# Attention and two expert layers: bias rows of 640 columns, fewer and respaced loads, and products of the identity in the first pair

## The chip, the core and the metric

One Trainium2 chip, one core. The metric is the device time of one launch in microseconds, the median over runs. Engines: TensorE (PE; PEld is its weight load), VectorE (DVE), ScalarE (ACT), GpSimd (POOL) and SyncE (SP), which here issues every DMA.

## What is computed

Attention with a bias made from relative positions, then two expert layers on the 2304 rows that it gives.

```python
# B, H, S, D = 4, 8, 576, 64; hidden 32
scores = q @ k.T / sqrt(D)
x = log1p(abs(i - j)) / log1p(max(i, 1))
bias = relu(x * w1 + b1) @ w2                   # [S, S, H], the same for every batch
attn = softmax(scores + bias) @ v
x = rows of attn                                # [B*S, H*D] = [2304, 512]
h = x @ w_in;  x = (h - tanh(h)) @ w_out        # 512 -> 2048 -> 512
out = (silu(x @ w_gate) * (x @ w_val)) @ w_out2 # 512 -> 1536 -> 512
```

## The kernel before

**Bias tables.** The bias depends on the position and the head alone, so it is made once, in 36 tiles (`bias_rows`, L146). A tile holds 16 positions x 8 heads on 128 partitions and 576 columns. Four operations make the hidden rows `r` (`bias_hidden`, L128): three on VectorE (L141), one on ScalarE (L143). TensorE multiplies them by `w2` (L163, L168), ScalarE evicts the tile into `bev` (L172, scaled; there are five `bev` buffers), and SyncE writes it to DRAM scratch (L177). The order of tiles is written out (`GEN_ORDER`): the last 64 positions come first. Once all tiles of a span of positions are made, and two more, `bias_load` (L179) reads them back, for a pair of heads, as a tile `bt` of 128 partitions x 2 x 576. The columns of the second head are turned by 64 (512 to 575 come first), so its row is read in two pieces; a span takes three DMAs.

**Pairs and units.** The work goes through 16 pairs (two heads, one batch) of five units (128 positions; the first unit of a pair, t = 4, has 64). `load` (L194) brings q, k and v of a pair in quarter rows of 64 numbers, with the last 64 positions in a tile `end`: three issues for q, six for k, four for v. `qk_transpose` (L223) turns q and k on TensorE, ScalarE copies the result out (L245, L250, L253) and q and k are split into a high and a low part (`qk_high`, ScalarE, L269; `qk_low`, GpSimd, L60).

**A unit.** Scores on TensorE (L306), softmax: bias and minimum on VectorE (L321), exponential on ScalarE (L332), `r` = 1/sum on VectorE (L341, L342; one buffer), scaling on GpSimd (L350). Three units later the probabilities are transposed (L372, L389) and copied out (L402); values are multiplied in L421 into the PSUM bank `x`, which the last four table tiles also use (banks a, b, c and x).

**The order** is written out. After the tables' first part (33 tiles; `run`, L440, where a list `extra` puts one piece of the first two pairs' loading and transposing ahead of each two tiles), each unit is a step, and strings give the order of a step's pieces on every engine: C is scores, S softmax, G a table tile, P and p transposes, V values, F and D copies out, N and M the norm and scaling, L the loads. Pair n's q and k are loaded at step 5n-9, its v at step 5n+1. SyncE issues in program order.

**Expert layers.** Weight pieces are loaded as raw words and prepared (class `Weights`). During attention this goes in rounds of ten steps (`ALONE_PARTS`, L706): `W` is `vector_second`, which ends by issuing the next load (L597). The expert layers are products of two-part numbers, three per product (L695).

Of the kernel before, what the change touches and what calls it, by code (L numbers as in the profile page):

```python
# [9 lines left out]
F32 = mybir.dt.float32  # L10
# [36 lines left out]
)  # L47
AV_END = {(0, 0): (6, (0, 1, 2, 3, 4)), (1, 0): (7, (0, 1, 2, 3, 4))}

FIRST_ORDER = "LuCpQSOGPqVFoGDNME"  # L50
STEP_ORDER = "LuXYCHSTGGPpVFDNME"
FOURTH_ORDER = "LuCHSTPpVFXDNYME"
END_ORDER = "NMuPpFDAuPpFDVXY"

LAG = 3
GEN_ORDER = [G for t in TORDER for G in range(8 * t, min(8 * t + 8, NG))]


# [4 lines left out]
class Attention:  # L63
# [34 lines left out]
    def bias_setup(self):  # L98
        nc = self.nc
        c = self.gen_p  # L100
        self.ident = self.const.tile([128, 128], F32, name="ident")
        make_identity(nc, self.ident)
        self.cst = c.tile([128, NCONST], F32, name="cst")
        nc.sync.dma_start(out=self.cst[:, TABW:NCONST], in_=self.packed[:, TABW:NCONST])
        half = 640
        nc.sync.dma_start(out=self.cst[:, 0:half], in_=self.packed[:, 0:half])
        nc.sync.dma_start(out=self.cst[:, half:TABW], in_=self.packed[:, half:TABW])
        b1c = self.cst[:, C_B1:C_B1 + 1]
        self.b1p = c.tile([128, NBLK], F32, name="b1p")
        nc.vector.tensor_scalar(self.b1p, self.cst[:, C_PSI:C_PSI + NBLK], b1c, None, ALU.mult)  # L110
        self.table(self.cst[:, 0:half])
        self.rest = self.cst[:, half:TABW]

        self.w2 = self.cst[:, C_W2:NCONST]
        self.nipsi = c.tile([128, NG], F32, name="nipsi")
        rows = self.packed.rearrange("(g r) c -> g r c", g=QG)
        blocks = c.tile([128, NBLK], F32, name="blocks")
        for j in range(4):
            at = slice(32 * j, 32 * j + 32)
            nc.sync.dma_start(out=blocks[at, :], in_=rows[:, 0:H, C_NIPSI:C_NIPSI + NBLK])  # L120
            nc.gpsimd.tensor_copy(self.nipsi[at, :], blocks[at, j::4])
        self.scratch = [self.dram.tile([n * H, S], F32, name=f"bias_{t}") for t, (_, n) in enumerate(SPANS)]

    def table(self, t):

# [20 lines left out]
    def bias_rows(self, G):  # L146

        nc = self.nc
        n = GEN_ORDER.index(G)
        if n == 0:  # L150
            self.bias_hidden(G)
        if n + 1 < NG:
            self.bias_hidden(GEN_ORDER[n + 1])
        R = self.R.pop(G)
        if self.ps_gen:
            both = (self.ps_gen if n % 2 else self.ps_s).tile([128, 2, 512], F32, tag="s", name=f"bps_{G}")
            ps = both[:, 0, :], both[:, 1, :]
        else:
            both = None
            ps = [self.bank(tag, f"bps{tag}_{G}") for tag in ("cx" if n % 2 else "ab")]  # L160

        for j in range(4):
            nc.tensor.matmul(  # L163
                ps[0][32 * j:32 * j + 32].rearrange("p (t n) -> p n t", t=4), self.w2,
                R[j][:, 0:512].rearrange("p (n t) -> p n t", t=4), start=True, stop=True,
            )
        for j in range(4):
            nc.tensor.matmul(ps[1][32 * j:32 * j + 32, 0:64], self.w2, R[j][:, 512:S], start=True, stop=True)  # L168
        out = self.gen_p.tile([128, S], F32, tag="bev", name=f"bev_{G}", bufs=BEV_BUFS)
        ni = self.nipsi[:, G:G + 1]  # L170
        if both is not None:
            nc.scalar.activation(out, both.rearrange("p e n -> p (e n)")[:, 0:S], AF.Copy, scale=ni)  # L172
        else:
            nc.scalar.activation(out[:, 0:512], ps[0], AF.Copy, scale=ni)  # L174
            nc.scalar.activation(out[:, 512:S], ps[1][:, 0:64], AF.Copy, scale=ni)
        t, r0 = divmod(G, 8)
        nc.sync.dma_start(out=self.scratch[t][128 * r0:128 * r0 + 128, :], in_=out)  # L177

    def bias_load(self, hp, t):  # L179
        n = SPANS[t][1]  # L180
        bt = self.bias_p.tile(
            [128, n // 64, S], F32, tag=f"bias{n}", name=f"bt_{hp}_{t}", bufs=4 if n == 128 else 1,
        )
        src = self.scratch[t].rearrange("(q h) k -> q h k", h=H)

        for j in range(2):
            to = bt[:, j, :] if n == 128 else bt[64 * j:64 * j + 64, 0, :]
            for x, y, z in ((0, S, 0),) if j == 0 else ((64, S, 0), (0, 64, 512)):
                self.nc.sync.dma_start(out=to[:, x:y], in_=src[:, 2 * hp + j, z:z + y - x])
        self.bias_t[hp, t] = bt  # L190


# [1 line left out]
    def load(self, hp, b, nm):  # L194
        nc = self.nc
        a = {"q": self.q, "k": self.k, "v": self.v}[nm][b, 2 * hp:2 * hp + 2]
        t = self.nat.tile([128, 4, 2, D], F32, tag=nm, name=f"{nm}n_{hp}_{b}", bufs=2 if nm == "v" else 1)
        by4 = lambda j, x, y: a[j, x:y].rearrange("(p t) d -> p t d", t=4)
        for j in range(1 if nm == "k" else 2):
            nc.sync.dma_start(out=t[:, 0:4, j, :], in_=by4(j, 0, 512))  # L200
        if nm == "v":

            end = self.vend[self.nbuf["v"] % 2]
            self.nbuf["v"] += 1
            for j in range(2):
                nc.sync.dma_start(out=end[64 * j:64 * j + 64, j, :], in_=a[j, 512:576])
            self.nt[hp, b, nm] = t, end
            return

        if nm == "q":  # L210
            self.nt[hp, b, "end"] = self.nat.tile([128, 2, D], F32, tag="end", name=f"qkn_{hp}_{b}")
        end = self.nt[hp, b, "end"]
        if nm == "q":
            nc.sync.dma_start(out=end[64:128], in_=a[:, 512:576].rearrange("j p d -> p j d"))
        else:
            nc.sync.dma_start(out=end[0:64, 0, :], in_=a[0, 512:576])
            nc.sync.dma_start(out=t[0:64, 0, 1, :], in_=a[1, 512:576])
            nc.sync.dma_start(out=t[64:128, 0:4, 1, :], in_=by4(1, 0, 256))
            nc.sync.dma_start(out=t[0:64, 1:4, 1, :], in_=by4(1, 256, 512)[:, 0:3])
            nc.sync.dma_start(out=end[0:64, 1, :], in_=by4(1, 256, 512)[:, 3])  # L220
        self.nt[hp, b, nm] = t

    def qk_transpose(self, hp, b, which):  # L223

# [2 lines left out]
        ps = self.ps_s.tile([128, 2, 512], F32, tag="s", name=f"{which}T_{hp}_{b}")  # L227
        parts = [(slice(t, 256, 4) if which == "q" else slice(64 * t, 64 * t + 64), nat[:, t, :, :]) for t in range(4)]
        if which == "k":
            parts.append((slice(256, 320), self.nt.pop((hp, b, "end"))))  # L230
        for to, a in parts:
            for h in range(2):
                r = slice(64 * h, 64 * h + 64)
# [145 lines left out]
    def ends_t(self, u):  # L379
# [5 lines left out]
        for x in (t, t + 1):  # L385
# [2 lines left out]
            at = GROUP_OF[x][1]  # L388
            self.nc.tensor.transpose(self.pt_end[:, at:at + 128], both, self.ident)  # L389

    def probs_out(self, first):
        nc = self.nc
        t, half, (pt, pe), at, n = self.raw_pt
# [14 lines left out]
    def values(self, hp, b, z, cs):  # L408
# [8 lines left out]
        for c in cs:  # L417
            for j in range(2):
                r = slice(64 * j, 64 * j + 64)
                lhs, rhs = (v[:, c, j, :], pt[:, c, j, :]) if c < 4 else (end[:, j, :], pe)  # L420
                nc.tensor.matmul(ps[r, 0:n], lhs, rhs, start=c == 0, stop=c == 4)  # L421
        if 4 not in cs:
            return
# [16 lines left out]
    def run(self, early, aside):  # L440
# [18 lines left out]
        for n, p in enumerate(pairs[1:], 1):  # L459
            preps[5 * n - 5] = p  # L460
            if n > 1:
                loads.setdefault(max(5 * n - 9, 2), []).extend([(*p, "q"), (*p, "k")])
            loads.setdefault(5 * n + 1, []).append((*p, "v"))
        gens = list(GEN_ORDER)
        due = []
# [20 lines left out]
        for which in "qk":  # L486
            extra.append(lambda which=which: (self.qk_transpose(*pairs[0], which), self.qk_raw(which)))
        extra += [self.qk_high, self.qk_low] * 2
        extra += [lambda: self.load(*pairs[0], "v")]
        extra += [lambda which=which: self.load(*pairs[1], which) for which in "qk"]  # L490
        gen(GEN0)
        while len(gens) > GEN_LATE:
            if extra:
                extra.pop(0)()
            gen(GEN_EACH)
        for f in extra:
            f()
        self.unit_banks()
        avs = {}
        for n, (hp, b) in enumerate(pairs):  # L500
# [32 lines left out]
        def next_turn(i):  # L533
# [6 lines left out]
            E=lambda i: at(self.expo, i), V=products, X=lambda i: self.values_high(), Y=lambda i: self.values_low(),  # L540
            Q=transposes("q"), q=transposes("k"), O=lambda i: self.qk_raw("q"), o=lambda i: self.qk_raw("k"),
            H=lambda i: i % 5 and i > 1 and self.qk_high(), T=lambda i: i % 5 and i > 1 and self.qk_low(), G=lambda i: gen(1),
            A=lambda i: aside(last - i),
        )
        for i in range(len(units) + 3):
            for a in END_ORDER if i > last else (FIRST_ORDER, STEP_ORDER, STEP_ORDER, FOURTH_ORDER, STEP_ORDER)[i % 5]:
# [18 lines left out]
class Weights:  # L565
# [79 lines left out]
    def vector_second(self):  # L645
        if p := self.second:

            w = p["bits"].bitcast(F32)
            self.nc.vector.scalar_tensor_tensor(w, p["m"], MIN_HIGH * MIN_HIGH, w, ALU.is_ge, ALU.mult)
        self.load()  # L650

    def scalar_third(self):
        if p := self.third:
# [21 lines left out]
    def part_of_step(self, now, n):  # L675
# [3 lines left out]
        for part in ALONE_PARTS[n]:  # L679
            dict(  # L680
                m=self.scalar_second, W=self.vector_second, h=self.scalar_third, l=self.pool_third,
                a=lambda: self.vector_first(0), r=self.scalar_first, b=lambda: self.vector_first(1), F=self.pool_first,
            )[part]()

    def due(self, now):
# [17 lines left out]
BEV_BUFS, GEN0, GEN_LATE, GEN_EACH = 5, 5, 4, 2  # L703
RAW_BUFS, POINT_AT = 2, -2
PACED, SOON = 74, 7
ALONE_PARTS = ("a", "", "h", "ml", "W", "b", "", "r", "F", "")  # L706
UNITS = [(0, 512), (512, 512), (1024, 512), (1536, 512), (2048, 256)]
ORDER, LAST_ORDER = (0, 1, 4, 2, 3), (0, 1, 2, 3, 4)

# [351 lines left out]
```

## Time and profile before

| | |
|---|---|
| Median of 3 runs | 1162.05 us (1160.62 to 1164.0) |
| Profiled execution | 1161.49 us |
| Its span in the trace | 1159.7 us, 20798 instructions |
| Granted TensorE clock, mean | 0.992 of full |
| Busy: PE, PEld | 1133.0 us (98%), 906.5 us (78%) |
| Busy: DVE, ACT, POOL | 818.9 us (71%), 700.3 us (60%), 541.3 us (47%) |
| DMA | 77.95 MB in 100103 packets, 63904 of them under 512 B |

The profile has a page of sums and views that can be cut to a stretch, an engine or a line. A busy time is a sum over the whole span; stages with different limits are in it together. Times in a timeline count from the span's start. What stands in brackets behind a row of a timeline is the engine's idle time before it and what ended it. The profiled execution is one run; its span leaves out what lies around the first and last instruction.

### The profile page before, as it was taken

The numbers are of one execution on the slowest core, as the hardware profiler recorded it, in microseconds if no ns is written. First come the engines' busy times: TensorE is split into PE (matmuls) and PEld (weight loads), VectorE is DVE, ScalarE is ACT, GpSimd is POOL, SyncE is SP. The second block draws the span as 40 slices with busy tenths as digits, with TensorE's granted clock in tenths as the row PEclk, the third lists the DMA queues.
The fourth block names the chain that finished last, engine by engine and source line by source line (L and its number), as shares of the span: only waits on it lengthen the run. The fifth ranks groups of instructions, "written<-read, shape, count | busy, mean of one in ns | idle before, by whom it ended". The sixth has DMA issues, their size and how long they took to land.

```text
span 1159.7 us, 20798 instructions
## 1 busy us (share of the span) xinstructions
PE 1133.0 (98%) x7624; PEld 906.5 (78%) x7624; DVE 818.9 (71%) x1592; ACT 700.3 (60%) x1439; POOL 541.3 (47%) x513
## 2 busy tenths in 40 slices
PE   7889999999999999999999999999999999999998
PEld 3367777777678888888888887888888888888887
DVE  7768998999698889799979978633664366343232
ACT  7788999999598877777868876411331233122111
POOL 1046777777455355355445748622552254233111
PEclk9979999999999999999999999999999999999999
DMA  5753636362111111111101201110121012100111
GB/s 182 247 160 89 167 86 161 86 166 61 29 55 56 37 55 56 37 37 49 61 19 38 62 31 55 56 36 1 39 79 48 1 56 71 37 9 11 37 63 65
DMA packets 100103, 77.95 MB, mean 67 GB/s; under 512 B 63904, under 2 KB 84640, under 8 KB 100000
## 3 DMA queue, kind: packets, MB, share of 16 engines
q1 hardware_dynamic: 100000, 76.61, 22.0%
q8 instruction: 60, 0.98, 0.4%
q14 instruction: 43, 0.35, 0.1%
HBM read 61.25 MB, written 15.34 MB: 66 GB/s over the span
## 4 chain that ended last, share of the span: by engine, by line
PE 89%; ACT 4%; DVE 3%; issue 1%; DMA 1%; SPq 1%; POOL 1%; ACTq 0%; DVEq 0%; POOLq 0%
PE h L695 16%; PE y L695 16%; PE val L695 13%; PE o L695 13%; PE gate L695 13%; PE x L421 7%; PE s L306 6%; PE pTa L372 2%; DVE r L141 1%; PE pTb L372 1%; PE bps L163 1%; PE pE L389 1%; ACT p L332 1%; ACT r L143 1%; PE kT L234 0%
## 5 line engine op out<-in xcount | busy, mean ns | idle before, releaser
L879 ACT ACTIVATE sq<-gate 128x512 f32<-128x512 f32 (+1 forms) x60 | 33.3, 555 | 328.8 <-PE gate L695 328.8
L60 POOL TENSOR_TENSOR gl<-g,gh 128x512 fp32r<-128x512 f32 (+1 forms) x67 | 82.5, 1231 | 248.9 <-ACT gh L830 187.6
L885 DVE TENSOR_TENSOR sq<-gate,sq 128x512 f32<-128x512 f32 (+1 forms) x60 | 38.3, 638 | 189.9 <-ACT sq L879 189.9
L350 POOL TENSOR_SCALAR p<-p,r 128x576 f32<-128x576 f32 x144 | 109.4, 771 | 112.7 <-ACT bev L174 60.1
L695 PE MATMUL y<-gh,whi 128*128 128x512 f32 (+1 forms) x428 | 140.1, 370 | 2.5 <-POOL gh L60 1.2
L695 PE MATMUL h<-xh,whi 128*128 128x512 f32 (+1 forms) x320 | 118.1, 369 | 0.0
L695 PE MATMUL h<-xl,whi 128*128 128x512 f32 (+1 forms) x320 | 117.9, 368 | 0.0
L695 PE MATMUL h<-xh,wlo 128*128 128x512 f32 (+1 forms) x320 | 117.7, 368 | 0.0
L695 PE MATMUL y<-gh,wlo 128*128 128x512 f32 (+1 forms) x320 | 117.7, 368 | 0.0
L332 ACT ACTIVATE p<-p,m 128x576 f32<-128x576 f32 x144 | 111.1, 774 | 1.2 <-DVE m L321 0.9
L321 DVE CUSTOM_DVE_ANT_0 p<-s,bt 128x576 f32<-128x576 f32 x144 | 103.6, 753 | 11.0 <-PE s L306 10.8
L695 PE MATMUL o<-whi,gh 128*128 128x512 f32 x288 | 103.5, 389 | 0.0
L60 POOL TENSOR_TENSOR gh<-g,gh 128x512 fp32r<-128x512 f32 (+1 forms) x33 | 39.4, 1195 | 126.2 <-ACT gh L830 96.7
L695 PEld LDWEIGHTS y<-gh,whi 128*128 128x128 f32 x428 | 79.2, 188 | 17.2 <-POOL gh L60 1.5
L695 PE MATMUL val<-xh,whi 128*128 128x512 f32 (+1 forms) x240 | 88.4, 368 | 1.1 <-DVE g L823 1.1
L695 PE MATMUL val<-xl,whi 128*128 128x512 f32 (+1 forms) x240 | 88.3, 368 | 0.0
L695 PE MATMUL gate<-xl,whi 128*128 128x512 f32 (+1 forms) x240 | 88.3, 368 | 0.0
L695 PE MATMUL val<-xh,wlo 128*128 128x512 f32 (+1 forms) x240 | 88.3, 368 | 0.0
L695 PE MATMUL gate<-xh,wlo 128*128 128x512 f32 (+1 forms) x240 | 88.3, 368 | 0.0
L695 PE MATMUL gate<-xh,whi 128*128 128x512 f32 (+1 forms) x240 | 88.2, 368 | 0.0
L804 ACT ACTIVATE sq<-h 128x512 f32<-128x512 f32 (+1 forms) x80 | 44.3, 554 | 72.2 <-PE h L695 72.2
L695 PE MATMUL o<-wlo,gh 128*128 128x512 f32 x216 | 84.1, 390 | 0.0
(152 smaller groups left out, 3197.5 us busy)
## 6 DMA issues: line engine op xcount, KB each, us to landing
raw_out<-in_moe_w_out_dram SPq DMA_DIRECT2D x28, 512.0 KB, 3.5
bias<-bev SPq DMA_DIRECT2D x36, 288.0 KB, 2.5
raw_in<-in_moe_w_in_dram SPq DMA_DIRECT2D x16, 512.0 KB, 3.7
raw_gate<-in_moe_w_gate_dram SPq DMA_DIRECT2D x12, 512.0 KB, 3.7
raw_val<-in_moe_w_val_dram SPq DMA_DIRECT2D x12, 512.0 KB, 3.5
bt<-bias SPq DMA_DIRECT2D x16, 288.0 KB, 4.2
out_dram<-acc SPq DMA_DIRECT2D x18, 256.0 KB, 2.0
qn<-in_q_dram SPq DMA_DIRECT2D x32, 128.0 KB, 2.8
```

The costliest lines, as they stand in the source:

```text
L60: (engine or nc.gpsimd).tensor_tensor(out, a, b, ALU.subtract)
L141: nc.vector.tensor_scalar(r, src, b1, 0.0, ALU.add, ALU.max)
L306: nc.tensor.matmul(self.st[u][j][:, e, 0:HALF], lhs, k[r, y, e * HALF:(e + 1) * HALF], start=n == 0, stop=n == 2,)
L321: nc.vector.tensor_tensor_reduce(out=p[:, n, :].rearrange("p (e f) -> p e f", e=2), in0=ps[n][:, :, 0:HALF], in1=bt[:, n, :].rearrange("p ...
L332: nc.scalar.activation(p[:, n, :], p[:, n, :], AF.Exp, bias=m[:, n:n + 1], scale=-1.0, accum_out=ls[:, n:n + 1],)
L350: nc.gpsimd.tensor_scalar(p[:, n, :], p[:, n, :], r[:, n:n + 1], 1.0, ALU.mult, ALU.mult)
L372: nc.tensor.transpose(half[h][:, 64 * m:64 * m + 64], p[r, j, k:k + 128], self.ident[r, r])
L421: nc.tensor.matmul(ps[r, 0:n], lhs, rhs, start=c == 0, stop=c == 4)
L695: nc.tensor.matmul(out, lhs[a], rhs[b], start=first and n == 0, stop=last and n == 2)
L804: nc.scalar.activation(u, h, AF.Square)
L879: self.nc.scalar.activation(self.tmp(it, "sq"), it["p"][0], AF.Sigmoid)
L885: nc.vector.tensor_tensor(it["sq"], gate, it["sq"], ALU.mult)
```

## The change

- A table tile gets 640 columns: GpSimd copies its last 64 in front (behind the eviction, ahead of the write), and scratch rows are 640 wide. The two heads' rows then follow each other in the right order, and `bias_load` takes one DMA for a span of 128 positions, two for the last of 64.
- v comes in rows of 256 numbers, one issue for both heads (three issues with its end). The end of k lies in k's own tile, which is allocated with q's loads (five issues for k).
- In the list `extra` an empty turn stands ahead of the second pair's q, and another ahead of its k.
- Where a step loads q and k of one pair and v of another, v now comes last.
- A new piece I, behind V, multiplies the 128x128 identity by itself four times into bank x, in steps 1 to 5.
- While attention runs, the next weight load is issued two steps later in the round (part `L`), and no more in `vector_second`.

```diff
-FIRST_ORDER = "LuCpQSOGPqVFoGDNME"
-STEP_ORDER = "LuXYCHSTGGPpVFDNME"
-FOURTH_ORDER = "LuCHSTPpVFXDNYME"
+FIRST_ORDER = "LuCpQSOGPqVIFoGDNME"
+STEP_ORDER = "LuXYCHSTGGPpVIFDNME"
+FOURTH_ORDER = "LuCHSTPpVIFXDNYME"
...
+FILL_STEPS, FILL = (1, 2, 3, 4, 5), 4
...
-        self.scratch = [self.dram.tile([n * H, S], F32, name=f"bias_{t}") for t, (_, n) in enumerate(SPANS)]
+        self.scratch = [self.dram.tile([n * H, S + 64], F32, name=f"bias_{t}") for t, (_, n) in enumerate(SPANS)]
...
-        out = self.gen_p.tile([128, S], F32, tag="bev", name=f"bev_{G}", bufs=BEV_BUFS)
+        row = self.gen_p.tile([128, S + 64], F32, tag="bev", name=f"bev_{G}", bufs=BEV_BUFS)
+        out = row[:, 64:S + 64]
...
+        nc.gpsimd.tensor_copy(row[:, 0:64], row[:, S:S + 64])
         t, r0 = divmod(G, 8)
-        nc.sync.dma_start(out=self.scratch[t][128 * r0:128 * r0 + 128, :], in_=out)
+        nc.sync.dma_start(out=self.scratch[t][128 * r0:128 * r0 + 128, :], in_=row)
...
-        src = self.scratch[t].rearrange("(q h) k -> q h k", h=H)
-
-        for j in range(2):
-            to = bt[:, j, :] if n == 128 else bt[64 * j:64 * j + 64, 0, :]
-            for x, y, z in ((0, S, 0),) if j == 0 else ((64, S, 0), (0, 64, 512)):
-                self.nc.sync.dma_start(out=to[:, x:y], in_=src[:, 2 * hp + j, z:z + y - x])
+
+        x = 2 * hp * (S + 64) + 64
+        src = self.scratch[t].rearrange("(q h) k -> q (h k)", h=H)[:, x:x + 2 * S]
+        if n == 128:
+            self.nc.sync.dma_start(out=bt.rearrange("p j k -> p (j k)"), in_=src)
+        else:
+            for j in range(2):
+                self.nc.sync.dma_start(out=bt[64 * j:64 * j + 64, 0, :], in_=src[:, j * S:j * S + S])
...
         if nm == "v":
+            t = self.nat.tile([128, 2, 4, D], F32, tag="v", name=f"vn_{hp}_{b}", bufs=2)
+            nc.sync.dma_start(
+                out=t.rearrange("p j t d -> p j (t d)"), in_=a[:, 0:512].rearrange("j (p t) d -> p j (t d)", t=4),
+            )
...
+            t = self.nt[hp, b, "q"] = self.nat.tile([128, 4, 2, D], F32, tag="q", name=f"qn_{hp}_{b}")
+
+            k = self.nt[hp, b, "k"] = self.nat.tile([128, 5, 2, D], F32, tag="k", name=f"kn_{hp}_{b}")
+            for j in range(2):
+                nc.sync.dma_start(out=t[:, :, j, :], in_=by4(j, 0, 512))
+            nc.sync.dma_start(out=k[64:128, 4], in_=a[:, 512:576].rearrange("j p d -> p j d"))
+            return
+        t = self.nt[hp, b, "k"]
+        nc.sync.dma_start(out=t[:, 0:4, 0, :], in_=by4(0, 0, 512))
+        nc.sync.dma_start(out=t[0:64, 4, 0, :], in_=a[0, 512:576])
+        nc.sync.dma_start(out=t[0:64, 0, 1, :], in_=a[1, 512:576])
+        nc.sync.dma_start(out=t[64:128, 0:4, 1, :], in_=by4(1, 0, 256))
+        nc.sync.dma_start(out=t[0:64, 1:5, 1, :], in_=by4(1, 256, 512))
...
+    def fill(self, i):
+        if i in FILL_STEPS:
+            ps = self.bank("x", f"fill_{i}")
+            for _ in range(FILL):
+                self.nc.tensor.matmul(ps[:, 0:128], self.ident, self.ident, start=True, stop=True)
...
+        for n, p in enumerate(pairs[1:], 1):
             loads.setdefault(5 * n + 1, []).append((*p, "v"))
...
-        extra += [lambda: self.load(*pairs[0], "v")]
-        extra += [lambda which=which: self.load(*pairs[1], which) for which in "qk"]
+        extra += [lambda: self.load(*pairs[0], "v"), None]
+        extra += [lambda: self.load(*pairs[1], "q"), None, lambda: self.load(*pairs[1], "k")]
...
-        self.load()
+        if not self.polite:
+            self.load()
...
-ALONE_PARTS = ("a", "", "h", "ml", "W", "b", "", "r", "F", "")
+ALONE_PARTS = ("a", "", "h", "ml", "W", "b", "L", "r", "F", "")
```

## Rows read from the trace of the kernel before

**Rows 1.** The page: granted clock in 40 slices, and the write of a table tile.

```profile
PEclk9979999999999999999999999999999999999999
...
bias<-bev SPq DMA_DIRECT2D x36, 288.0 KB, 2.5
```

**Rows 2.** Stages: length, busy us (instructions) of PE, PEld, DVE, ACT, POOL; clock, DMA.

```profile
20.00:45.00 25.00, 24.73 (x288) 11.40 (x278) 24.59 (x57) 24.95 (x40) 0.00 (x0) 1.00 0.71 235
45.00:54.60 9.60, 5.13 (x58) 1.99 (x50) 5.53 (x13) 4.27 (x7) 0.00 (x0) 1.00 0.74 244
...
61.20:72.30 11.10, 9.58 (x120) 6.31 (x118) 7.50 (x23) 10.34 (x25) 2.31 (x3) 0.99 0.46 165
72.30:85.40 13.10, 11.26 (x102) 9.67 (x104) 8.82 (x24) 9.57 (x25) 9.54 (x14) 0.50 0.53 132
...
94.50:109.00 14.50, 14.50 (x193) 10.62 (x191) 12.58 (x40) 12.97 (x34) 10.18 (x13) 1.00 0.28 63
```

**Rows 3.** Waits of TensorE (PE), 0 to 92 us: total, times, longest.

```profile
PE bps L163 <- ACT r L143: 4.8, 3, 2.7
```

**Rows 4.** ScalarE's timeline: the evictions of table tiles 15, 26, 27 and 31.

```profile
30.64 0.74 ACT L172 ACTIVATE bev<-bps,nipsi 128x576 f32<-128x576 f32 x1
...
45.20 0.73 ACT L172 ACTIVATE bev<-bps,nipsi 128x576 f32<-128x576 f32 x1
...
49.44 0.74 ACT L172 ACTIVATE bev<-bps,nipsi 128x576 f32<-128x576 f32 x1 [2.84 <-DMA bias<-bev]
...
58.64 0.74 ACT L172 ACTIVATE bev<-bps,nipsi 128x576 f32<-128x576 f32 x1 [0.51 <-PE bps L168]
```

**Rows 5.** SyncE's timeline, the loads and the write of tile 22.

```profile
42.46 0.56 SPq L200 DMA_DIRECT2D kn<-in_k_dram  x1
...
46.85 0.53 SPq L177 DMA_DIRECT2D bias<-bev  x1
```

**Rows 6.** The chain that ended last, 61 to 92 us: start, us, what.

```profile
61.26 0.98 PE s L306 x6
...
76.76 1.81 PE s L306 x6
...
80.51 0.57 ACT pt L402
...
81.12 0.69 ACT kraw L250
...
84.65 1.79 PE x L421 x8
86.44 0.99 PE s L306 x9
...
90.33 1.23 PE x L421 x8
```

**Rows 7.** Waits of TensorE, 92 to 560 us, and the chain near 200 us.

```profile
PE kT L234 <- DMA qkn<-in_k_dram: 1.0, 1, 1.0
...
197.03 3.34 DMA qkn<-in_k_dram
```

**Rows 8.** GpSimd (POOL) beside VectorE (DVE): the two timelines, 5 to 8 us.

```profile
5.36 1.53 POOL L121 COPY nipsi<-blocks 32x36 f32<-32x36 f32 x4 [4.06 <-DMA blocks<-in_packed_dram]
...
7.41 0.97 POOL L456 MEMSET vend<- 128x128 f32 x2
...
5.01 1.38 DVE L141 TENSOR_SCALAR r<-cst,b1p 128x576 f32<-128x576 f32 x3
...
6.70 1.53 DVE L141 TENSOR_SCALAR r<-cst,b1p 128x576 f32<-128x576 f32 x3
```

**Rows 9.** The same two engines' timelines at 74 us.

```profile
74.41 1.37 DVE L341 TENSOR_SCALAR r<-l 128x2 f32<-128x2 f32 x1 [0.88 <-POOL p L350]
...
74.35 1.41 POOL L60 TENSOR_TENSOR k<-kraw,k 128x576 fp32r<-128x576 f32 x1
```

**Rows 10.** ScalarE's timeline: the last table tile's second bank is read.

```profile
68.28 0.31 ACT L175 ACTIVATE bev<-bpsx,nipsi 128x64 f32<-128x64 f32 x1
```

More of the change, by code (lines that the diff above doesn't have):

```diff
@@ L196, in load @@
         a = {"q": self.q, "k": self.k, "v": self.v}[nm][b, 2 * hp:2 * hp + 2]
[L197 to L200, printed above, removed]
         if nm == "v":
+            t = self.nat.tile([128, 2, 4, D], F32, tag="v", name=f"vn_{hp}_{b}", bufs=2)
+            nc.sync.dma_start(
+                out=t.rearrange("p j t d -> p j (t d)"), in_=a[:, 0:512].rearrange("j (p t) d -> p j (t d)", t=4),
+            )
             end = self.vend[self.nbuf["v"] % 2]
@@ L208, in load @@
             return
+        by4 = lambda j, x, y: a[j, x:y].rearrange("(p t) d -> p t d", t=4)
         if nm == "q":
[L211 to L221, printed above, removed]
+            t = self.nt[hp, b, "q"] = self.nat.tile([128, 4, 2, D], F32, tag="q", name=f"qn_{hp}_{b}")
[10 more added lines that the diff above has]
+        nc.sync.dma_start(out=t[0:64, 1:5, 1, :], in_=by4(1, 256, 512))
     def qk_transpose(self, hp, b, which):
@@ L229, in qk_transpose @@
         if which == "k":
-            parts.append((slice(256, 320), self.nt.pop((hp, b, "end"))))
+            parts.append((slice(256, 320), nat[:, 4, :, :]))
         for to, a in parts:
@@ L419, in values @@
                 r = slice(64 * j, 64 * j + 64)
-                lhs, rhs = (v[:, c, j, :], pt[:, c, j, :]) if c < 4 else (end[:, j, :], pe)
+                lhs, rhs = (v[:, j, c, :], pt[:, c, j, :]) if c < 4 else (end[:, j, :], pe)
                 nc.tensor.matmul(ps[r, 0:n], lhs, rhs, start=c == 0, stop=c == 4)
@@ L488, in run @@
         extra += [self.qk_high, self.qk_low] * 2
-        extra += [lambda: self.load(*pairs[0], "v")]
-        extra += [lambda which=which: self.load(*pairs[1], which) for which in "qk"]
+        extra += [lambda: self.load(*pairs[0], "v"), None]
+        extra += [lambda: self.load(*pairs[1], "q"), None, lambda: self.load(*pairs[1], "k")]
         gen(GEN0)
         while len(gens) > GEN_LATE:
-            if extra:
-                extra.pop(0)()
+            if extra and (f := extra.pop(0)):
+                f()
             gen(GEN_EACH)
-        for f in extra:
-            f()
         self.unit_banks()
@@ L542, in run @@
             H=lambda i: i % 5 and i > 1 and self.qk_high(), T=lambda i: i % 5 and i > 1 and self.qk_low(), G=lambda i: gen(1),
-            A=lambda i: aside(last - i),
+            A=lambda i: aside(last - i), I=self.fill,
         )
@@ L681, in part_of_step @@
                 m=self.scalar_second, W=self.vector_second, h=self.scalar_third, l=self.pool_third,
-                a=lambda: self.vector_first(0), r=self.scalar_first, b=lambda: self.vector_first(1), F=self.pool_first,
+                a=lambda: self.vector_first(0), r=self.scalar_first, L=self.load, b=lambda: self.vector_first(1), F=self.pool_first,
             )[part]()
```

## The prediction, made before the changed kernel was run

> **What bounds the kernel now.** I read the page first. In its 40 slices TensorE's granted clock is near full in all but the third, from 58 to 87 us [rows 1]. So I cut the first 109 us into stages and read each one's busy time [rows 2]. From 20 to 45 us the bias tables are made: VectorE (24.59 of 25 us) and ScalarE (24.95) are full. From 45 to 54.6 us every engine is half idle. From 61.2 us the first attention units run; between 72.3 and 85.4 us TensorE has a granted clock of 0.50, the lower level, and is still idle for 1.8 us. From 94.5 us a pair of heads takes 14.5 us with TensorE busy in all of it: from there on only work on TensorE costs time, and whatever the first 94 us gain or lose arrives at the end in full.
>
> The hole at 45 us: the waits of TensorE name ScalarE's `r` [rows 3], and ScalarE itself waits, in its timeline, for the DMA that writes `bev` [rows 4]. Twelve evictions from 30.64 to 45.20 stand 1.32 us apart; the next five take until 58.64, 2.69 us each. The cause stands on SyncE's queue [rows 5]: from 42.46 on come the six loads of `k`, and the next table's write is issued only at 46.85. That tile is the 22nd of 36, and with five `bev` buffers the 27th eviction, at 49.44, has to wait until it has landed.
>
> In the first units I read the chain that ended last [rows 6]. The same six score products take 0.98 us at 61.26 and 1.81 us at 76.76; eight value products take 1.79 us at 84.65 and 1.23 us at 90.33. The scores of unit 7 start at 86.44, 25.2 us after those of unit 0.
>
> Later one wait for a load is left: `kT` waits 1.0 us for the last piece of `k`, which lands at 200.4 us [rows 7]. That is where the bias tiles of the next heads, `v`, q and k stand behind each other on SyncE.
>
> **The change, part by part.**
>
> *Fewer and spaced loads.* A pair's q, k, v loads go from 13 issues to 11, five bias tiles from 15 to 6, and the 256-byte rows of `v` become rows of 1 KB. For the hole the order counts: q now goes out ahead of tile 22, k ahead of tile 26, with one empty turn before each. A `bev` buffer comes round every 5 x 1.32 = 6.6 us. Of that, eviction takes 0.74 [rows 4], the new copy some 0.38 (below), issue up to 0.53 [rows 5] and landing 2.5 [rows 1], which leaves 2.45 us. Six k issues take 42.46 to 46.85, 0.73 us each [rows 5]; five take 3.6. They begin when tile 25 is written, about 1.3 us before tile 26 is ready, so its write is 2.3 us late: inside the slack, narrowly. q's three issues (2.2 us) and the single bias load behind tile 22 fit too. So the whole excess goes, 58.64 - 45.20 - 5 x 1.32 = **6.8 us** [rows 4]. Lower bound: half, 3.4, if writes that share the DMA engines with the 256-byte rows of q and k still land late.
>
> *640-column rows.* GpSimd copies 64 columns of each tile between eviction and write. This lengthens the path of the write (what waits behind it on SyncE are the next loads), and it puts GpSimd beside a full VectorE. The trace has no such copy. The nearest row is L121, four copies of 32x36, 1.53 us in all; beside them three VectorE operations of L141 take 1.38 us. The three at 6.70, with wider memsets beside them, take 1.53 [rows 8]. So a GpSimd operation delays VectorE by 0 to 0.15 us. The far bound is the whole operation: at 74.41 a VectorE instruction on 128x2 lasts 1.37 us and ends just after a GpSimd subtraction of 1.41 us that began at 74.35 [rows 9]. I take 0.03 us a copy, near the first rows, since 64 columns are nearer to 36 than to the memsets' 128 and 256: 33 tiles ahead of the first unit make **1.0 us lost**. The bounds are 0 and 16 us, the latter with 0.485 us, half of the two memsets at 7.41. The Trainium skill ("SBUF — State Buffer", "Who interferes with whom") says that against a VectorE operation in a two-port mode "the other fully blocks" for a whole instruction. By that rule VectorE would lose each copy entirely; rows 9 agree, the first pair of rows 8 does not. The write also carries 11% more bytes, some 0.2 us of a landing of 2.5.
>
> *The products of the identity.* Four a step in five steps, on TensorE behind the step's own work; nobody reads them. Price: the eight value records are four instructions over 320 columns, 1.23 us at the full clock [rows 6]. If two of them run beside each other on half the array, one alone costs 0.62 us; the identity fills the array, so 0.62 x 128/320 x 4 = 0.98 us a step (0.49 if width costs nothing). In steps 2 to 5 this lies in TensorE's wait for VectorE and ScalarE. In step 1 it does not: bank x holds the last table tile until L175 ends at 68.59 [rows 10], so the products start there, and the scores of unit 2 queue behind them; I estimate 1.4 us. That is given back at unit 4: its softmax stands behind an instruction that ends at 75.8 because of GpSimd's work on the next pair [rows 9], whatever the scores do. From 76.76 the chain runs to 86.44 on TensorE at the lower clock, 8.2 of 9.7 us, the rest being two copies on ScalarE at 80.51 and 81.12 [rows 6]. By the two pairs of [rows 6] the full clock takes (0.98 + 1.23)/(1.81 + 1.79) = 0.61 of the lower one's time, so 8.2 falls to 5.0: **3.2 us gained**, if the clock holds, and unit 7 starts 22.0 us after unit 0. Bounds: 5 gained (seven steps at the later 14.5/5 = 2.9 us each) and 5 lost (a rival, below).
>
> *Order of the loads.* q and k now go ahead of `v` where they share a step, and a bias tile is one issue: the wait at 200 us goes [rows 7], **1.0 us** (0 to 1.4). `v` passes behind eight issues, at 0.73 us some 6 us, and is used five steps, 14.5 us, later. The early weight loads move by two steps within a round of ten; their reader stands four steps, 11.6 us, behind, so nothing. The first expert item loads nothing and the item behind it does; what it would have loaded is not due for many items.
>
> **The sum.** 6.8 + 3.2 + 1.0 - 1.0 = 10.0 us off the profiled execution's 1161.49 (its span is 1159.7, the rest lies around it): 1151.5. The median of the runs shown is 0.56 above that execution, so **1152.0**.
>
> **The rivals.** A difference under 0.3% (3.5 us) can't be told from no change.
>
> *GpSimd blocks VectorE (the other side).* Place: the 33 table tiles, where VectorE is full. Without copies the gain is 11.0 us, so at 11.0/33 = 0.33 us lost to each copy all of it is gone; from 0.44 the kernel is slower by over 3.5 us. At 0.485 us it is 16 us lost: 1167. For it: rows 9. Against it: rows 8, where three of L141 end in 1.38 us beside copies. It is what the page named above would make of the copies. Chance 0.12, half of it past 0.44.
>
> *The products don't hold the clock.* They would take 2 us a step, ahead of the next scores in steps 3 to 5; with each unit's own products at the lower clock too, unit 7 starts about 30.4 us after unit 0, 5.2 later than now. 6.8 + 1.0 - 1.0 - 5.2 = 1.6 gained: 1160. For it: from 61.2 to 72.3 us TensorE was busy 9.58 of 11.1 us, and the clock fell all the same. Against: it is the idle time between them that the products fill, and a stretch with 11.26 of 13.1 us busy ended with the clock back [rows 2]. Chance 0.08.
>
> *Half of the hole stays.* The slack at tile 26 is 0.15 us; late landings, a slower issue of the merged rows or a late copy would use it up. 10.0 - 3.4 = 6.6: 1155.5. Chance 0.13.
>
> The forecast keeps 0.67. **Faster** by over 0.3%: 0.67 + 0.13, less 0.01 for the tail of the latter: 0.79. **Slower**: 0.06, and 0.01 for causes not seen: 0.07. **Same**: 0.06 + 0.08 = 0.14. The range goes from 1148 (the hole, 5 us in the units, 1.4 us late, copies free: 13.2 us, and rounding) to 1160, which takes in half a hole and the cold products; a blocked VectorE and the tails are left out.
>
> **What would show it.** Right: evictions every 1.32 us through the 33rd tile, with no wait for `bev`'s DMA; a granted clock of 1.00 from 45 us on; twenty products in five groups of about 1 us; unit 7's scores some 22 us behind unit 0's; no wait of `kT` for a load near 200 us; three L141 in 1.38 us beside a copy. Wrong: L141 spread to 1.5 us and more, and evictions every 1.45 us or slower (the copies); a granted clock of 0.5 after unit 3 (the products); a stall at tiles 27 to 31 (the loads); or scores of unit 2 held back by the products' bank for longer than unit 4 waits anyway.

## The result, and the profile after

The changed kernel takes 1152.43 us, the median of four runs (1152.35 to 1153.37), against 1162.18 for the kernel before in four: a ratio of 0.9917, interval 0.9900 to 0.9935. The forecast was 1152.0 with 1148 to 1160. The profiled execution took 1153.37 us, the slowest of its four, and its span went from 1159.7 to 1151.6 us.

The page and the windows of the changed kernel, with the stages that [rows 1] and [rows 2] show of before:

```profile
span 1151.6 us, 20876 instructions
...
PEclk9999999999999999999999999999999999999999
...
bias<-bev SPq DMA_DIRECT2D x36, 320.0 KB, 3.4
```

```profile
20.00:45.00 25.00, 24.67 (x277) 12.29 (x272) 24.07 (x55) 24.64 (x39) 8.15 (x17) 1.00 0.77 265
45.00:54.60 9.60, 8.48 (x95) 3.79 (x91) 7.69 (x18) 7.80 (x13) 2.14 (x6) 1.00 0.91 284
54.60:61.20 6.60, 6.60 (x81) 4.03 (x81) 5.60 (x14) 6.02 (x11) 1.85 (x4) 1.00 0.97 314
61.20:72.30 11.10, 9.96 (x119) 7.84 (x113) 6.80 (x21) 10.38 (x27) 6.52 (x10) 1.00 0.68 216
72.30:85.40 13.10, 13.10 (x178) 10.31 (x176) 10.98 (x34) 10.98 (x28) 10.04 (x13) 1.00 0.47 108
```

The kernel before, from 54.6 to 61.2 us:

```profile
54.60:61.20 6.60, 6.41 (x59) 3.33 (x59) 4.05 (x9) 5.39 (x9) 0.00 (x0) 0.74 0.75 256
```

The granted clock is 1.00 in every stage (before, it was 0.74 from 54.6 to 61.2 us and 0.50 from 72.3 to 85.4), TensorE is busy in all of 72.3 to 85.4 us, and the hole at 45 us has shrunk: TensorE 8.48 of 9.6 us there, 5.13 before. Two things are new. The DMA engines are busy 0.91 and 0.97 of the time from 45 to 61 us (the share is the last column but one; before, it was 0.74 and 0.75), and a table tile's write lands 3.4 us after its issue in the median, no longer 2.5.

What is left of the hole is seen in ScalarE's timeline (evictions of tiles 26, 27 and 28) and in the chain that ended last (start, us, what), where the write of tile 23 stands:

```profile
46.48 0.73 ACT L176 ACTIVATE bev<-bps,nipsi 128x576 f32<-128x576 f32 x1
...
47.87 0.74 ACT L176 ACTIVATE bev<-bps,nipsi 128x576 f32<-128x576 f32 x1
...
51.07 0.74 ACT L176 ACTIVATE bev<-bps,nipsi 128x576 f32<-128x576 f32 x1 [1.79 <-DMA bias<-bev]
```

```profile
44.41 6.55 DMA bias<-bev
```

Tile 28 takes the buffer of tile 23. That tile's write was issued in time, at 44.41, and landed 6.55 us later; up to some 4.8 us would have held nobody up. Before, the write itself was issued late [rows 5]. This wait has changed from SyncE's queue to the transfers.

SyncE's queue is close behind, though. Its timeline around the five loads of `k`:

```profile
46.91 0.71 SPq L226 DMA_DIRECT2D kn<-in_k_dram  x1
...
50.43 0.60 SPq L230 DMA_DIRECT2D kn<-in_k_dram  x1
51.14 4.33 SPq L182 DMA_DIRECT2D bias<-bev  x5
```

They take 4.1 us, and the write of tile 26, whose copy had ended at 47.82, goes out 3.3 us late, at 51.14. Tile 31, which takes its buffer, does not wait here because tile 28 has already held the tiles up.

The chain through the first units, beside [rows 6]:

```profile
57.68 0.98 PE s L315 x6
...
65.11 1.16 PE fill L404 x8
66.27 1.03 PE s L315 x11
...
73.91 0.80 PE s L315 x6
...
76.14 1.09 PE fill L404 x8
77.22 1.05 PE s L315 x12
...
78.82 1.23 PE x L436 x8
80.05 0.99 PE s L315 x12
```

Unit 0's scores start at 57.68 (61.26 before), unit 7's at 80.05 (86.44): 22.4 us instead of 25.2. The eight value products take 1.23 us where they took 1.79.

Where the 8.1 us of the span came from, by the same events in both traces: the first eviction is 0.5 us later (8.70 before, 9.16 after; in run 9 below, the same changed kernel, it is at 8.53, so the change is not the cause), unit 0's scores are 3.6 us earlier, unit 7's 6.4 us, the transposes of the pair at 176.80 us 6.5 us, those of the pair at 206.19 us 7.7 us, the first output products at 726.7 us 7.6 us. So it is 4.1 us in the tables, 2.8 us in the first units and 1.2 us near 200 us; the last 0.5 us lies behind the final products, and its cause was not looked for.

### The profile page after: what moved, and what is told of

Same layout as the page of the kernel before. It is cut to its first block, busy times and chain, and to the rows that moved or that the text cites. A ratio compares the mean times of both kernels' runs of the same rounds, so it can differ in the third digit from the quotient of the medians.

```text
span 1151.6 us, 20876 instructions
## 1 busy us (share of the span) xinstructions
PE 1131.4 (98%) x7664; PEld 907.8 (79%) x7664; DVE 819.1 (71%) x1592; ACT 701.6 (61%) x1439; POOL 558.5 (48%) x549
## 3 DMA queue, kind: packets, MB, share of 16 engines
q1 hardware_dynamic: 82272, 77.79, 22.3%
## 4 chain that ended last, share of the span: by engine, by line
PE 90%; ACT 3%; DVE 2%; issue 2%; DMA 1%; POOL 1%; SPq 0%; POOLq 0%; ACTq 0%; DVEq 0%
PE h L710 17%; PE y L710 16%; PE val L710 13%; PE o L710 13%; PE gate L710 13%; PE x L436 7%; PE s L315 6%; PE pTa L381 2%; PE pTb L381 1%; DMA bias<-bev 1%; ACT p L341 1%; PE pE L398 1%; DVE p L330 1%; PE bps L166 1%; POOL bev L180 1%
```

## The experiments

Ratios are to the kernel before, run beside each on the same chip. Their intervals are some 0.2% wide to either side, so what is said of single terms rests on the marks in the traces, named in each case.

**1. Without the products.**

```diff
-FILL_STEPS, FILL = (1, 2, 3, 4, 5), 4
+FILL_STEPS, FILL = (), 4
```

> The changed kernel without the twenty products of the identity. Theory (the products hold the clock): the granted clock falls to 0.5 within units 3 to 6 again, unit 7's scores start about 25 us after unit 0's (22.4 with the products), and the time is some 2.8 us above the changed kernel, about 1155. Rival (the clock fell only in the wake of the hole at 45 us, which is now shorter): the clock stays at 1.00, unit 2 no longer waits behind products, unit 7 starts 21 to 22.4 us after unit 0, and the time is 1151.5 to 1152.5.

Measured: 1155.19 us, ratio 0.9935 (0.9915 to 0.9954). Windows of that run:

```profile
60.00:66.00 6.00, 5.16 (x65) 3.19 (x61) 4.26 (x13) 5.90 (x15) 1.65 (x4) 1.00 0.63 242
66.00:72.00 6.00, 4.89 (x50) 4.01 (x50) 4.24 (x13) 5.56 (x17) 4.85 (x6) 0.70 0.78 210
72.00:78.00 6.00, 4.59 (x43) 3.92 (x43) 4.31 (x14) 3.84 (x10) 2.93 (x4) 0.50 0.26 55
78.00:84.00 6.00, 5.95 (x63) 4.66 (x63) 2.63 (x8) 4.47 (x11) 4.65 (x7) 0.66 0.43 103
```

The clock falls to 0.50 as before, though the hole ahead of it is small, and unit 7 starts 25.3 us after unit 0 (57.27 to 82.61). The products hold the clock; the rival falls.

**2. Without the empty turns.**

```diff
-        extra += [lambda: self.load(*pairs[0], "v"), None]
-        extra += [lambda: self.load(*pairs[1], "q"), None, lambda: self.load(*pairs[1], "k")]
+        extra += [lambda: self.load(*pairs[0], "v")]
+        extra += [lambda: self.load(*pairs[1], "q"), lambda: self.load(*pairs[1], "k")]
```

> The changed kernel without the two empty turns: v, q and k ahead of tiles 18, 20 and 22 as before, with the new, fewer issues. Theory (what counts is how many issues stand in a row on SyncE): the hole is back in good part, the excess over 1.34 us a tile is 4 to 5 us where the changed kernel has 2.2, the time about 1155. Rival (the DMA engines' throughput alone sets it, and the same bytes go out either way): excess within 0.5 us of the changed kernel's, time 1152.5 or a little under.

Measured: 1156.9 us, ratio 0.9952 (0.9935 to 0.9969). ScalarE's timeline, evictions 27 and 28, and SyncE's, the writes around the loads:

```profile
47.93 0.74 ACT L176 ACTIVATE bev<-bps,nipsi 128x576 f32<-128x576 f32 x1 [1.53 <-DMA bias<-bev]
...
52.41 0.74 ACT L176 ACTIVATE bev<-bps,nipsi 128x576 f32<-128x576 f32 x1 [3.08 <-DMA bias<-bev]
```

```profile
40.15 1.02 SPq L182 DMA_DIRECT2D bias<-bev  x2
41.22 0.56 SPq L226 DMA_DIRECT2D kn<-in_k_dram  x1
...
44.70 0.54 SPq L182 DMA_DIRECT2D bias<-bev  x1
...
45.83 4.14 SPq L182 DMA_DIRECT2D bias<-bev  x5
```

The two waits add to 4.6 us. Behind them TensorE's granted clock falls (its row from 54 to 60 us: busy, clock, DMA):

```profile
54.00:60.00 6.00, 6.00 (x51) 0.53 0.63 219
```

So the next tiles are late too: the 33rd eviction starts at 61.17, where it was 61.29 before the change and 57.78 after it. The spacing is worth nearly all that the hole gave back; the fewer issues without it, with the wide rows beside them, are worth next to nothing there. The time came out nearly 2 us above the 1155 expected; the wait's second cost, the clock, was not in that sum. It stood in the trace of before too (0.74 from 54.6 to 61.2 us).

The two waits differ. Tile 22's write went out at 44.70, behind all five `k` loads, and landed 3.1 us later. Tile 23's went out at 45.83 and landed only some 6.5 us later, by the end of tile 28's wait. So the empty turns do two things, keeping the queue free and spreading the transfers, and this run doesn't separate them.

**3. Rows of 576 columns.** No copy, and three DMAs a bias tile, as before the change:

```diff
-        nc.gpsimd.tensor_copy(row[:, 0:64], row[:, S:S + 64])
-        nc.sync.dma_start(out=self.scratch[t][128 * r0:128 * r0 + 128, :], in_=row)
+        nc.sync.dma_start(out=self.scratch[t][128 * r0:128 * r0 + 128, :], in_=out)
...
+        for j in range(2):
+            to = bt[:, j, :] if n == 128 else bt[64 * j:64 * j + 64, 0, :]
+            for x, y, z in ((0, S, 0),) if j == 0 else ((64, S, 0), (0, 64, 512)):
+                self.nc.sync.dma_start(out=to[:, x:y], in_=src[:, 2 * hp + j, z:z + y - x])
```

> The changed kernel with the table rows of before: 576 columns, no GpSimd copy, three DMAs for a bias tile. Theory (what is left of the hole is the DMA engines' throughput): with 11% fewer bytes written tile 28 waits under 1 us (1.8 with 640 columns), the first unit starts some 1 us earlier, of which 0.5 us is the copies' cost to VectorE; then up to 1 us is given back where bias loads of the next heads stand ahead of q and k near 190 us, so 1151.5 to 1152.5. Rival (SyncE's issues): two more issues behind tile 22 delay the next writes by 0.9 us, tile 28 waits 2.5 us or more, and the time is 1153.5 or more.

Measured: 1150.93 us, ratio 0.9903 (0.9882 to 0.9924). No tile up to the 30th waits; the 31st does, for 1.6 us. Unit 0 starts at 55.97, 1.7 us earlier than in the profile of the changed kernel; 0.7 us of that is that profile's late start (first eviction at 9.16, here at 8.49), so 1.0 us belongs to the edit. The eviction of tile 31, and the write of tile 26 in the chain that ended last:

```profile
53.43 0.74 ACT L175 ACTIVATE bev<-bps,nipsi 128x576 f32<-128x576 f32 x1 [1.61 <-DMA bias<-bev]
```

```profile
50.92 2.42 DMA bias<-bev
```

This wait is SyncE's queue again and not the transfers. Tile 26 was evicted by 45.67, but its write goes out at 50.92, behind the five `k` loads (45.91 to 50.82), and then lands in 2.42 us. The rival had the right queue and the wrong place. From 34 to 56 us the DMA engines are busy 0.83 of the time (0.93 in the changed kernel). Wide rows and the single bias DMA together bring nothing that shows here: the ratio is below that of the changed kernel, though the intervals overlap. Since both were taken back at once, this run doesn't say which of the two made tile 23's write land late. Near 190 us no wait came back, although a bias tile has its three issues again.

**4. v ahead of q and k.**

```diff
-        for n, p in enumerate(pairs[1:], 1):
-            loads.setdefault(5 * n + 1, []).append((*p, "v"))
+            loads.setdefault(5 * n + 1, []).append((*p, "v"))
```

> The changed kernel with v ahead of q and k again where they share a step. Theory (the order of the loads removed the wait of the transposed k near 200 us): TensorE waits about 1 us for a load of k once more, near 192 us, and the time is 1 to 1.2 us above the changed kernel, 1153.5. Rival (one issue for a bias tile was enough): no such wait, time 1152.4.

Measured: 1153.4 us (1151.44 to 1153.74), ratio 0.9920 (0.9898 to 0.9942). The waits of TensorE from 92 to 290 us, to be read against [rows 7]:

```profile
PE kT L243 <- DVE m L330: 1.1, 4, 0.3
PE x L436 <- DVE xl L451: 0.2, 1, 0.2
```

No wait for a load. With run 3 that says: with the rest of the change in place, the wait near 200 us stays away without one issue a bias tile (run 3), and in this profile without q and k ahead of v. Two other parts stood in both runs, fewer issues for v and k and the later weight load; no run took those out, so what removes the wait is open. Nor is the time settled. This run's profiled execution, with tile waits of 0.44 and 0.60 us only, is 2 us under its three other runs, and those lie at 1153.4 to 1153.7, near the 1153.5 of the theory; they have no trace, so whether the wait came back in them is not shown. How long the tiles wait differs from execution to execution.

**5. Three copies a tile.**

```diff
-        nc.gpsimd.tensor_copy(row[:, 0:64], row[:, S:S + 64])
+        for _ in range(3):
+            nc.gpsimd.tensor_copy(row[:, 0:64], row[:, S:S + 64])
```

> The changed kernel with GpSimd's copy of the 64 columns made three times for each tile. Theory (a copy beside VectorE's table work costs VectorE only 0.02 to 0.03 us; the spacing of tiles 14 to 22 went from 1.326 to 1.351 us with one): two more copies raise it to 1.39 to 1.41 us a tile, 1.3 to 1.8 us over 33 tiles, and the write of a tile starts about 1 us later, so the wait for a buffer near tile 28 can grow by as much: time 1153.5 to 1155.5. Rival (GpSimd's operation shuts VectorE out for its whole length, 0.24 to 0.55 us): 1.85 us a tile or more, 16 us more, time near 1168.

Measured: 1152.8 us, ratio 0.9930 (0.9908 to 0.9952). Evictions 14 and 22 of this run:

```profile
28.91 0.73 ACT L176 ACTIVATE bev<-bps,nipsi 128x576 f32<-128x576 f32 x1
...
39.75 0.74 ACT L176 ACTIVATE bev<-bps,nipsi 128x576 f32<-128x576 f32 x1
```

That is 10.84 us for eight tiles, 1.355 each. With one copy it is 1.351 (29.96 to 40.77), with none 1.326 before, and the same 1.326 in run 3 (29.02 to 39.63). So the first copy, or the wider row that comes with it, costs 0.025 us a tile, and two more cost 0.004. The rival asked for 1.85, and my theory for 1.39 to 1.41: both are missed, and the time is below the 1153.5 of my theory too. What the 0.025 is stays open, since no run had the wide rows without a copy. GpSimd pays instead of VectorE: in its timeline of the changed kernel a copy takes about 0.24 or about 0.55 us (0.64 at most).

```profile
24.77 0.24 POOL L180 COPY bev<-bev 128x64 f32<-128x64 f32 x1 [1.86 <-ACT bev L176]
26.18 0.55 POOL L180 COPY bev<-bev 128x64 f32<-128x64 f32 x1 [1.17 <-ACT bev L176]
```

**6. The products alone**, on the kernel before (piece I in the three orders, and its function):

```diff
+    def fill(self, i):
+        if i in FILL_STEPS:
+            ps = self.bank("x", f"fill_{i}")
+            for _ in range(FILL):
+                self.nc.tensor.matmul(ps[:, 0:128], self.ident, self.ident, start=True, stop=True)
```

> The kernel before with the twenty products of the identity and nothing else of the change. Theory (the parts add up): the hole at 45 us stays as it was, first unit's scores at 61 us; the granted clock stays at 1.00 from then on, unit 7's scores start 22.4 us after (25.2 before), the wait near 200 us stays: time 2.8 us under the kernel before, ratio 0.9976. Rival (the products only help once the hole is gone): the clock falls in units 3 to 6 all the same, unit 7 starts 25 us or more after unit 0, ratio 1.000 or above.

Measured: 1159.28 us, ratio 0.9981 (0.9969 to 0.9993). The hole is that of before (waits of 2.94 and 2.36 us at tiles 27 and 28), the granted clock is 1.00 from 61.6 us on, and unit 7 starts 22.9 us after unit 0 (61.63 to 84.49), 0.4 us of it a wait for `k` at unit 5. The wait of `kT` near 200 us stays, 1.0 us. The parts add up.

**7. Rows of 576, q a turn earlier.**

```diff
-        extra += [lambda: self.load(*pairs[0], "v"), None]
-        extra += [lambda: self.load(*pairs[1], "q"), None, lambda: self.load(*pairs[1], "k")]
+        extra += [lambda: self.load(*pairs[0], "v")]
+        extra += [lambda: self.load(*pairs[1], "q"), None, None, lambda: self.load(*pairs[1], "k")]
```

> Rows of 576 columns (as in the run with the rows of before), with q one turn earlier and k behind two empty turns, so that q no longer goes out just ahead of the bias load behind tile 22. Theory (what is left of the hole is transfers that pile up on the DMA engines): no wait at tiles 23 to 31 over 0.5 us, 1.0 to 1.6 us under the run with 576 columns: about 1149.5. Rival (the bytes up to tile 31 are the same, so the wait only moves): a wait of 1 us or more at tiles 20 to 31, time 1150.5 to 1151.5.

Measured: 1151.35 us, ratio 0.9918 (0.9898 to 0.9937). Tile 31 still waits 1.4 us, and the time is the rival's. The place of q was not the cause. Nor are the bytes: as in run 3 the write of tile 26 goes out behind the five `k` loads (46.25 to 50.75), and lands soon:

```profile
50.84 2.46 DMA bias<-bev
```

**8. Rows of 576, products in steps 2 to 5.**

```diff
-FILL_STEPS, FILL = (1, 2, 3, 4, 5), 4
+FILL_STEPS, FILL = (2, 3, 4, 5), 4
```

> Rows of 576 columns and the products in steps 2 to 5 alone, without those of step 1. Theory (the 2.2 us for which step 1's products hold unit 2's scores back are given back at unit 4, which waits for GpSimd anyway): unit 7 starts within 0.4 us of 22.3 us after unit 0, time 1150.5 to 1151, clock at 1.00. Rival 1 (what step 1 costs isn't given back): unit 7 starts 1 us or more earlier, 1149.5. Rival 2 (step 1's products are needed for the clock): the clock falls in units 2 to 6, 1152 to 1154.

Measured: 1151.4 us, 0.4 above the expected range, ratio 0.9922 (0.9900 to 0.9944). Unit 2's scores start 6.4 us after unit 0's, not 8.5 as in run 3, but unit 7's 22.1 us after, not 22.3. The granted clock of the profiled execution is 0.999 in the mean. What step 1's products delay is given back, all but 0.2 us.

**9 and 10. The changed kernel again, and with q and k in rows of 1 KB.** The second has the same issues and bytes; q and k land at other places of their tiles, so its attention is that of wrongly ordered q and k. One of its five edits:

```diff
-                nc.sync.dma_start(out=t[:, :, j, :], in_=by4(j, 0, 512))
+                nc.sync.dma_start(
+                    out=t[:, 2 * j:2 * j + 2].rearrange("p t j d -> p (t j d)"),
+                    in_=by4(j, 0, 512).rearrange("p t d -> p (t d)"),
+                )
```

> The changed kernel itself once more, beside the three that follow, for their comparison. If tiles 23 to 31 wait for transfers whose landing differs from execution to execution, their wait is again somewhere between 0.7 and 2.2 us and the runs spread over some 2 us; the median lies near 1152.4.

> The changed kernel with the same number of issues and bytes for q and k, but in rows of 1 KB instead of 256 bytes, which puts them at other places of their tiles (the attention is computed on wrongly ordered q and k). Theory (the packets of 256 bytes keep the DMA engines busy, and the writes of the tables land late behind them): landings of bev fall back to 2.5 to 3 us in the median and 4.5 at most (3.4 and 6.8 now), no tile waits over 0.3 us, first unit's scores 1 to 2 us earlier, time 1150.5 to 1151.5. Rival (bytes alone: 320 KB a tile and bias tiles fill the engines): waits and landings as in the changed kernel, 1152.4.

Measured: 1152.38 us, ratio 0.9922 (0.9907 to 0.9937), and 1152.23 us, ratio 0.9922 (0.9903 to 0.9940). The DMA view from 34 to 56 us, first of run 9, then of run 10:

```profile
DMA packets 5304, 6.89 MB, mean 313 GB/s; under 512 B 2880, under 2 KB 3136, under 8 KB 5300
...
q1 hardware_dynamic: 5300, 6.84, 92.5%
```

```profile
DMA packets 3855, 7.04 MB, mean 320 GB/s; under 512 B 847, under 2 KB 1615, under 8 KB 3851
...
q1 hardware_dynamic: 3851, 7.00, 91.5%
```

With less than a third of the small packets the engines are as busy, tile 28 waits 1.63 us, where run 9 has 1.80, and the writes land in 3.2 us in the median and 6.9 at most (3.4 and 6.7 in run 9). My theory of the small packets falls. What is left is the bytes, at 313 to 320 GB/s, but no run changed them alone. A rival stands in both runs: the single load of a bias tile, 576 KB, is issued directly ahead of tile 23's write.

**11 and 12. Rows of 576 with q and k in halves; then also their low parts on VectorE.** `load` gets a `part` that picks one half's issues, and `qk_low` of the second pair another engine:

```diff
-        extra += [lambda: self.load(*pairs[0], "v"), None]
-        extra += [lambda: self.load(*pairs[1], "q"), None, lambda: self.load(*pairs[1], "k")]
+        extra += [lambda: self.load(*pairs[0], "v")]
+        extra += [lambda nm=nm, part=part: self.load(*pairs[1], nm, part) for nm in "qk" for part in range(2)]
...
+        eng = nc.vector if self.ps_gen or max(self.nbuf["q"], self.nbuf["k"]) <= 2 else nc.gpsimd
```

> Rows of 576 columns, and the second pair's q and k each in two halves, one half ahead of each two tiles, instead of empty turns. Theory (what is left is the pile of small packets behind q and k): the wait of 1.6 us at tile 31 goes, no tile waits over 0.5 us, first unit's scores near 54.5 us, time near 1149.5, under both the changed kernel and the run with 576 columns. Rival (the bytes up to tile 31 decide): a wait of 1 us or more stays, time 1150.5 to 1151.

> As the run before, with the low parts of the second pair's q and k on VectorE instead of GpSimd. Theory (unit 4's softmax waits for GpSimd, which is why step 1's products cost nothing): unit 4's softmax starts 0.7 to 1.2 us earlier (now 14.76 us after unit 0's scores), then held by the load of the last bias tile; unit 7 starts 21.2 to 21.8 us after unit 0, 0.6 to 1 us off the time. Rival (another engine holds unit 4): no difference over 0.3 us.

Measured: 1151.07 us (1150.05 to 1152.07), ratio 0.9910 (0.9895 to 0.9926), and 1152.52 us, ratio 0.9923 (0.9907 to 0.9940). In run 11's profiled execution the hole is gone: one wait of 0.26 us, unit 0 at 53.9 us, a span of 1148.3. Then 0.6 us go to a wait of `kT` for a `k` load at unit 5. In run 12, with the same loads, tiles 28 and 30 wait 0.67 and 0.60 us. So the halves shorten the wait; they don't exclude it. I had blamed a pile of small packets; SyncE's queue is reason enough, since with the halves at most three `k` loads stand between two writes, where run 3 has five. Run 11's median is 1.3 us under that of the changed kernel run beside it (run 9), and run 3's is as low. The intervals overlap: a version that beats both kernels is likely here, but these runs don't settle it.

In run 12 unit 4's softmax comes 15.7 us after unit 0's scores, 0.9 us later than in run 11. VectorE's timeline tells why: the subtractions for q and `k` now stand on VectorE itself, the one for `k` ahead of unit 4's softmax (71.21).

```profile
69.37 0.92 DVE L62 TENSOR_TENSOR k<-kraw,k 128x576 fp32r<-128x576 f32 x1
70.21 0.41 DVE L420 COPY pt<-pTb 128x256 f32<-128x256 f32 x1
...
71.21 0.76 DVE L333 CUSTOM_DVE_ANT_0 p<-s,bt 128x576 f32<-128x576 f32 x1
```

So this run could not tell whether GpSimd holds unit 4; it put another holder in its place.

## Why the prediction was right, and where its terms were off

The sum was 10.0 us; the medians differ by 9.75, the two spans by 8.1. By the prediction's own list one sign of being wrong came, a stall at tiles 27 to 31, and its first sign of being right, no wait for `bev`'s DMA, did not. Term by term:

*Fewer and spaced loads, 6.8 us: too much.* Tiles 26 to 31 now take 8.6 us (46.48 to 55.08) instead of 13.44, and tile 23 waits 0.3: some 4.5 us went. The step that failed is the slack, in the words "landing 2.5 ... which leaves 2.45 us". The 2.5 was the median of a kernel whose DMA engines were busy only 0.74 of that stretch. In the changed kernel landings have a median of 3.4 and one of 6.55 us ahead of tile 28. I had this in the lower bound and in a rival ("late landings"), but named the 256-byte rows as its cause; run 10 refutes that, and leaves bytes or the bias load ahead of the write. The lengthening of the writes by 11%, which I put at 0.2 us and dropped, may belong to this term: run 3, without it and without the single bias load, has no wait before tile 31. "Five take 3.6" failed too: the five `k` issues took 4.1 us here and 4.9 in run 3, and the write of tile 26 was 3.3 us late and not 2.3. In runs 3 and 7 this is the wait that is left, so a landing of 2.5 us alone would not have saved the term. Of the old hole, the write of tile 22 issued late and landing in 2.50 us shows SyncE's queue as the cause; run 2 shows that the spacing removes it, though not by the queue alone.

*640-column rows, 1.0 us lost: right.* 0.025 us a tile over 33 tiles is 0.8 us; whether the copy or the wider row costs it stays open. The slower rival, GpSimd blocking VectorE, is refuted by run 5. The two-port rule of the Trainium skill ("SBUF — State Buffer", "Who interferes with whom") gives the shared ports, against a VectorE operation in a two-port mode, to whichever engine issues first, and the other waits; that VectorE's table operations are in such a mode no run shows. The rule fits GpSimd's side here, whose copy takes 0.55 us at times and 0.24 at others; the measured spacing of the tiles (0.025 us more with one copy) shows that VectorE hardly waits in its turn. The better evidence was the copies of [rows 8], not the long case of [rows 9].

*Products, 3.2 us gained: 2.8.* The mechanism held in both directions: alone they bring 2.3 us in the traces, 2.7 without the wait for `k` (run 6), and without them the clock falls (run 1). Their price is 1.09 us a step in the chain, where I had 0.98. Unit 2's scores come 2.2 us later against unit 0's than before, not 1.4, because the wait for bank x is 1.0 us on top of the products. TensorE's timeline, unit 2's scores before, then the products of step 1 after:

```profile
67.59 1.55 PE L306 MATMUL s<-k,q 64*128 64x288 f32 x12
```

```profile
65.11 1.16 PE L404 MATMUL fill<-ident 128*128 128x128 f32 x8 [1.03 <-ACT bev L179]
```

The 1.4 was not worked out from rows; the bank free at 68.59, 0.98 us of products and this start at 67.6 would have given some 2.0. Of the 2.2 us, 0.2 stays (run 8). Unit 4's softmax starts 14.8 us after unit 0's scores, 14.7 before (VectorE's timeline, before and after):

```profile
75.93 0.76 DVE L321 CUSTOM_DVE_ANT_0 p<-s,bt 128x576 f32<-128x576 f32 x1
```

```profile
72.44 0.76 DVE L330 CUSTOM_DVE_ANT_0 p<-s,bt 128x576 f32<-128x576 f32 x1
```

That the delay is given back by then is measured. That GpSimd is what gives it back was read from the trace and stays argued (run 12).

*Order of the loads, 1.0 us: 1.2, the part that does it open.* The wait near 200 us is gone, and run 6 shows that the products don't remove it. I had named the order and the single bias issue as one step; in the traces neither was needed by itself (runs 3 and 4), and fewer issues or the later weight loads may do it.

By the marks the change is worth 8.1 us of span, 1.9 less than the sum; the first term alone is 2.3 short. The medians still differ by 9.75 because the profiled execution of before lay 0.7 us under its median and that of after 0.9 above its own. The mechanisms were right; the agreement within half a microsecond on the median is partly luck.

## What to carry to other kernels

Where writes and loads share one issuing queue, count what stands in a row between two writes against the slack of their buffers, and take the landing time from a stretch in which the DMA engines are as full as they will be, not from a median of the old kernel. Filling a queue's hole makes everything denser; the next limits here were late landings and, right behind them, the same queue at the next row of loads. Splitting such a row, so that writes go out between its parts, shortened the waits to 0.26 us in run 11's profile, and to 1.27 us in all in run 12's. A few products that nobody reads are worth having where TensorE would otherwise idle into its lower clock, provided that the bank they write to is free.

## What the runs showed of the hardware that I had not expected

Rows of 1 KB instead of 256 bytes, at equal issues and nearly equal bytes (7.04 against 6.89 MB in the 22 us), hardly changed the DMA engines' busy share (91.5 against 92.5%) or the wait behind them (1.63 against 1.80 us). Three GpSimd copies a tile beside a VectorE that is busy nearly all the time cost the tiles' pace only 0.004 us more than one. And a stall can cost twice: in run 2 the waits for buffers, 4.6 us, were followed by a granted clock of 0.53, near the lower of TensorE's two levels, from 54 to 60 us, with TensorE busy in all of it.
